# An attention and MLP kernel on one core: PV sums kept per pair of visits, their bank shared with QK, and a new order of maxima and exps

## The chip, the core and the metric

The kernel runs on one core of one Trainium2 chip. The metric is the device time of one launch in microseconds (us), as the median of several runs. The engines are called by the profile's names: PE is TensorE's matmul side and PEld its weight loads, DVE is VectorE, ACT is ScalarE, POOL is GpSimd, SP is SyncE, which issues nearly all DMAs.

## What is computed

The input is x of 2048 rows and 512 columns, in float32. It is normalised row by row, and two things are made of the result: attention with 32 heads of width 16, and a dense block of width 1792 with a squared ReLU. The second gates the first:

```python
xn = _layernorm(x, axis=-1)
s = _A_ref(xn, A_wqkv, A_wo)                # softmax(q k^T / 4) v, then wo
g = _silu(_B_ref(xn, B_w1, B_b1, B_w2, B_b2))   # relu(xn w1 + b1)^2 w2 + b2
return x + s * g
```

The attention is by far the larger part: 32 heads of 2048 by 2048 scores, which need a row maximum, an exp and a product with v. Most matmul operands are kept as a high and a low part, so that a product is three matmuls.

## The kernel before

**Units and steps.** The attention is cut into 32 units (`NU`): a unit is four heads (one "quad") by one chunk of 512 queries. A unit has 16 steps, one for each block of 128 keys. In a step, PE makes four score tiles of 128 keys by 512 queries (one for each head; `exp_mm`, matmul L1337), ACT turns each into exps (L1349, tile `pt`), and two steps later the PV matmuls (`pv_mm`, L453) multiply the exps by v. Since the exps need a row maximum that is known before, PE also makes every score tile a second time, transposed, 24 steps ahead (`LEAD`): `max_mm`, matmul L367, reduced by DVE (L374). These two kinds are called QK here, "s" for the exps' and "m" for the maxima's. So each step has four of each.

**Two lanes.** A QK matmul uses 64 of the array's 128 rows. Its partner on the other 64 rows ("lane" 0 or 1) is a matmul of the dense block (L268), made in the same way half by half, so that QK and dense matmuls run side by side. PV matmuls use all rows and 32 columns each, four side by side.

**Long slots.** `long_slots` writes out four steps by hand: 28 rounds, numbered r0 to r27, and three visits to PV. In 24 rounds a QK matmul on one lane stands beside a dense one on the other; first the 12 dense units of lane 0, then the 12 of lane 1. In the four rounds of `DOUBLE` both lanes hold QK. The string `ORDERS` tells which QK is "s" and which is "m". `VISITS` puts one step of PV after r11, one after r15 and two after r27. I call the rounds between the visits A (r0 to r11), B (r12 to r15) and C (r16 to r27). Between these blocks of four steps stand short slots, of one step, seven rounds and one step of PV, at the places where a dense sum does not divide by four.

**The fence.** Both lanes of a dense sum add into the same PSUM bank `pd_t`, and must not do so at once. So after the last dense unit of lane 0, in r12, `fence` (L1677) puts a wait into ACT's instructions: it waits for that matmul and sets a semaphore, on which lane 1's first dense matmul, in r15, waits. On ACT the fence stands behind whatever was issued before it, the exp of r12's own QK included, if that QK is an "s".

**Banks.** PSUM has eight banks of 128 by 512. Three (`se`) and three (`pm_t`) serve QK, one (`pd_t`) the dense sum, one (`po`) PV. The PV bank collects the 16 steps of a unit; then `evac` (L463) copies it on ACT into the SBUF tile `ot`, and a chain of DMAs and POOL operations (L502 to L504, `evac_norm`) divides by the sums over 14 steps. POOL waits there for the DMA `hl<-r_d`. Which QK gets which of the six banks is settled when the program is written: `flow` keeps a rough clock of PE, ACT and DVE (`ROUND`, `STEP`, `VISIT`, `READERS`), and each QK takes the bank that this clock says is free first, by preference one that the same reader had. On the chip a QK's weight load waits until the bank's last reader is through.

**Order.** In the loop all engines run in the order in which the code issues. POOL squares and splits the dense block's ReLU output (L618, L109, L110), splits the maxima and does `evac_norm`.

Of the kernel before, what the change touches and what calls it, by code (L numbers as in the profile page):

```python
# [9 lines left out]
F32 = mybir.dt.float32  # L10
F32R = mybir.dt.float32r
AF = mybir.ActivationFunctionType
# [50 lines left out]
READERS = {"s": (476, 675), "m": (600, 745), "d": (600, 755)}  # L63
EPS = 1e-5


# [1 line left out]
def kernel(  # L68
# [56 lines left out]
    with ExitStack() as ph:  # L125
# [136 lines left out]
        def block(mms, per, post, between={}):  # L262


            def emit(ms, lane, follow):
                r = slice(64 * lane, 64 * lane + 64)
                for out_, lh, rh, first_, last_ in ms:
                    mm = nc.tensor.matmul(  # L268
                        out_, lh(r), rh(r),
                        start=first_ and lane == 0, stop=last_ and lane == 1,  # L270
                        skip_group_check=True,
                    )
# [12 lines left out]
            assert len(units) == 12  # L285
            yield [
                [
                    lambda m=m, lane=lane, k=k: [
                        emit(m, lane, None if k else last_use[0]),
                        lane and k in between and between[k](),  # L290
                    ][0]
                    for k, m in enumerate(units)
                ]
                for lane in range(2)
            ], post, ORDERS[per == 1]

        def terms3(ps, terms):

# [37 lines left out]
        def flow_visit(n):  # L336
            flow["pe"] += VISIT + n * STEP
            flow["fresh"] = True

        def flow_take(kind):  # L340
            free = [i for i, spot in enumerate(spots) if spot[0] <= flow["pe"] and spot[2] == kind]
            at, t, _ = spots.pop(min(free or range(len(spots)), key=lambda i: spots[i][0]))
            flow["pe"] = max(flow["pe"], at)
            return t

        def flow_give(t, kind):
            every, held = READERS[kind]
            begin_ = max(flow[kind], flow["pe"] + READY)
            flow[kind] = begin_ + every
            spots.append([begin_ + held, t, kind])  # L350

        def flow_bank(kind):
            t = flow_take(kind)
# [94 lines left out]
                        ),  # L448
                    )

        def pv_mm(po, qd, kb, pts):
            for j in range(4):
                nc.tensor.matmul(  # L453
                    po[32 * j : 32 * j + 32, :],
                    vs[qd][:, (4 * kb + j) * VW : (4 * kb + j) * VW + 32], pts[j],
                    start=(kb == 0), stop=(kb == NT - 1), skip_group_check=True,
                )

        def evac(po, u):
            qd, qc = divmod(u, 4)  # L460
            cs = slice(qc * 512, (qc + 1) * 512)
            ot = sp.tile([P, 512], F32, name="ot", bufs=1)
            nc.scalar.activation(ot, po, AF.Copy)  # L463
            if u == NU - 3:
# [1073 lines left out]
        def pv_step(st, pts):  # L1538
            u, kb = divmod(st, 16)
            if kb == 0:  # L1540
                pos[0] = pv.tile([P, 512], F32, name="po")
            pv_mm(pos[0], u // 4, kb, pts)
            if kb == NT - 1:
                if u < NU - 2:
                    evac(pos[0], u)
                elif u == NU - 2:
                    unit_inner(pos[0])
                else:
                    unit_final(pos[0])

        def dense():
            mp = ExitStack()
# [111 lines left out]
                post()  # L1664
            max_end(g)

        def long_slots(st0, units, post, order):

            if not spots:
                flow_start((pe, "se", "s", 3), (pm, "pm_t", "m", 3))  # L1670
            todo = [[(st0 + k, j) for k in range(4) for j in (lane, lane + 2)] for lane in range(2)]
            for kb in range(st0, st0 + 4):
                pts.setdefault(kb, {})
            ops, st, pv_at = list(order), st0, st0 - 2

            def fence(mm):
                use = nc.scalar.nop()  # L1677
                tc.add_manual_dep(
                    use.ins, mm.ins.name,
                    mybir.DependencyInfo(  # L1680
                        mybir.DependencyClass.Sync, mybir.DependencyReason.DATA
                    ),
                    reason="the row tile is done with the bank",
                )
                last_use[0] = use

            def qk(lane):
                if ops.pop(0) == "m":
                    return max_mm(lane)
# [55 lines left out]
        for st_ in range(NU * 16):  # L1745
            if st_ < done:
                continue
            begin(st_)
            if st_ == FIRST:
                qs.close()  # L1750
            item = next(dn, None)
            if st_ == FIRST:

                for g in (LEAD, LEAD + 1):
                    max_end(g)
                for fn in last_store:
                    fn()
            if item is not None and len(item) > 2:
                assert st_ % 4 == 0
                long_slots(st_, *item)  # L1760
                done = st_ + 4
                to_visit[0] = st_ + 2
                continue
            wait = st_ >= LAST_MAX and item is not None and item[0] is not None and (st_ + flip[0]) % 2
            if item is not None and item[0] is not None:
                slot(st_, *item)
            else:

                plain_slot(st_)
                flip[0] += 1  # L1770
            shift_due(st_ + 1 + LEAD)
            if wait and (st_ - 2) % 16 != 15:
                continue
            for step in range(to_visit[0], st_ - 1):
                pv_step(step, pts.pop(step))
            flow_visit(st_ - 1 - to_visit[0])
            to_visit[0] = st_ - 1
        assert not [1 for it in stream for _ in it] and not left
        run_waiting(True)
        assert not waiting and next(dn, None) is None  # L1780
        flow["on"] = False
        for st_ in range(to_visit[0], NU * 16):
            pv_step(st_, pts.pop(st_))
        wstk.close()


# [24 lines left out]
```

## Time and profile before

| | us |
|---|---|
| median of 3 runs | 1616.87 |
| the runs | 1616.87, 1617.13, 1610.39 |
| profiled execution | 1610.35 |
| its span | 1608.6 |
| chain that ended last: matmul L453 (PV) | 30% of the span |
| the same, L268 (dense) | 13% |
| the same, L367 and L1337 on `pm_t` and `se` (QK) | 12%, 8%, 6% and 11% |

The granted clock of TensorE was full in all of the span. A row of the timeline gives the start and the length of an instruction or of several in a row (xN), both in us, the engine, the line, the operation, what it writes and reads, the shape, and in brackets how long the engine sat idle before and what ended that. A matmul on 64 rows is written 64\*128, one of PV 128\*32. The length of a matmul is modelled; the starts carry the argument. PV's matmuls are counted twice in the trace, 8 records for a step and 16 for two.

### The profile page before, as it was taken

The page shows a single profiled execution, that of the slowest core. Times are in us where ns is not written, and L with a number is a line of the kernel's source. Part 1 is how long each engine was busy: PE and PEld are TensorE (multiplying, and loading weights), DVE is VectorE, ACT ScalarE, POOL GpSimd, SP SyncE. Part 2 cuts the span into 40 slices and gives each one's busy share as a digit, 9 for nine tenths or more (in the row PEclk, how much of TensorE's full clock was granted, in tenths as well). Part 3 has the DMA queues.
Part 4 walks back from the last instruction along what each step waited for, and adds up shares of the span by engine and source line. Part 5 has one row for each costly group of instructions (what it writes and reads, how often), then busy time and mean ns, then how long its engine had stood idle before and what let it go on. Part 6 is the DMA issues. An engine that isn't in the chain of part 4 may idle for free.

```text
span 1608.6 us, 36225 instructions
## 1 busy us (share of the span) xinstructions
PE 1595.1 (99%) x13660; PEld 964.0 (60%) x13660; DVE 1345.8 (84%) x2307; ACT 1189.6 (74%) x2347; POOL 534.9 (33%) x610
## 2 busy tenths in 40 slices
PE   8999999999999999999999999999999999999998
PEld 7798665566546654665566456655665566545543
DVE  7486888888888888888888888888888888887764
ACT  7212777788778777887788778777877788778886
POOL 6436766233113311331133113311331134214621
PEclk9999999999999999999999999999999999999999
DMA  8977556435343433433434334433442253236755
GB/s 293 245 239 229 180 159 158 135 94 131 81 106 90 115 75 95 134 88 98 92 106 106 83 92 123 116 83 81 128 128 56 67 152 86 68 93 213 224 178 182
DMA packets 164174, 209.20 MB, mean 130 GB/s; under 512 B 59136, under 2 KB 79360, under 8 KB 162432
## 3 DMA queue, kind: packets, MB, share of 16 engines
q1 hardware_dynamic: 163856, 206.63, 46.4%
q8 instruction: 108, 1.77, 0.5%
q14 instruction: 66, 0.54, 0.1%
q10 hardware_dynamic: 144, 0.26, 0.0%
HBM read 148.90 MB, written 56.34 MB: 128 GB/s over the span
## 4 chain that ended last, share of the span: by engine, by line
PE 96%; DMA 1%; DVE 1%; issue 0%; SPq 0%; ACT 0%; POOL 0%; DVEq 0%
PE po L453 30%; PE pd_t L268 13%; PE pm_t L367 12%; PE se L1337 11%; PE se L367 8%; PE pm_t L1337 6%; PE pm_t L1206 4%; PE pd_t L236 4%; PE pm_t L236 2%; PE pd_t L1206 1%; PE se L1176 1%; PE se L1110 1%; PE pm_t L1297 0%; DVE mx L374 0%; PE se L236 0%
## 5 line engine op out<-in xcount | busy, mean ns | idle before, releaser
L374 DVE TENSOR_REDUCE mx<-pm_t 128x1 f32<-128x512 f32 x1236 | 799.2, 683 | 134.8 <-PE pd_t L268 82.4
L1349 ACT ACTIVATE pt<-se 128x512 f32<-128x512 f32 x1240 | 686.1, 606 | 182.8 <-PE pd_t L268 90.9
L374 DVE TENSOR_REDUCE mx<-se 128x1 f32<-128x512 f32 x795 | 528.5, 683 | 64.3 <-PE se L367 28.2
L1337 PE MATMUL se<-qe,ka 64*128 64x512 f32 x1346 | 530.4, 417 | 0.7 <-ACT pt L1349 0.7
L453 PE MATMUL po<-pt,v 128*32 128x512 f32 x3820 | 498.4, 602 | 0.2 <-DVE tsm L898 0.2
L367 PE MATMUL pm_t<-ka,qm 64*128 64x512 f32 x1236 | 480.4, 408 | 0.1
L1349 ACT ACTIVATE pt<-pm_t 128x512 f32<-128x512 f32 x666 | 388.9, 606 | 101.0 <-PE pd_t L268 58.5
L268 PE MATMUL pd_t<-xc,w1s 64*128 64x256 f32 x2352 | 328.8, 286 | 0.0
L1337 PEld LDWEIGHTS se<-qe,ka 64*128 64x128 f32 x1346 | 241.1, 184 | 137.1 <-ACT pt L1349 107.7
L367 PE MATMUL se<-ka,qm 64*128 64x512 f32 x795 | 310.6, 410 | 0.2
L268 PE MATMUL pd_t<-w2t,hT 64*128 64x512 f32 x1080 | 298.5, 408 | 0.0
L268 PEld LDWEIGHTS pd_t<-xc,w1s 64*128 64x128 f32 x2352 | 295.0, 186 | 0.0
L367 PEld LDWEIGHTS pm_t<-ka,qm 64*128 64x128 f32 x1236 | 222.9, 184 | 112.9 <-DVE mx L374 98.2
L1337 PE MATMUL pm_t<-qe,ka 64*128 64x512 f32 x695 | 283.6, 418 | 0.0
L453 PEld LDWEIGHTS po<-pt,v 128*32 128x32 f32 x3820 | 87.8, 108 | 158.7 <-issue 143.3
L268 PEld LDWEIGHTS pd_t<-w2t,hT 64*128 64x128 f32 x1080 | 180.9, 184 | 3.2
L367 PEld LDWEIGHTS se<-ka,qm 64*128 64x128 f32 x795 | 145.6, 184 | 51.5 <-DVE mx L374 36.0
L1337 PEld LDWEIGHTS pm_t<-qe,ka 64*128 64x128 f32 x695 | 126.3, 184 | 79.5 <-ACT pt L1349 64.4
L618 POOL TENSOR_TENSOR r<-r 128x512 f32<-128x512 f32 x56 | 58.2, 1039 | 321.1 <-ACT r L615 321.1
L502 POOL TENSOR_TENSOR ot<-ot,hl 128x512 f32<-128x512 f32 x27 | 34.7, 1286 | 154.5 <-DMA hl<-r_d 88.1
L637 POOL TENSOR_TENSOR u<-u,b_t 128x512 f32<-128x512 f32 x16 | 20.5, 1284 | 164.4 <-ACT u L636 164.4
L110 POOL TENSOR_TENSOR hT<-r,hT 128x512 fp32r<-128x512 f32 x56 | 72.5, 1295 | 4.7
(184 smaller groups left out, 1552.5 us busy)
## 6 DMA issues: line engine op xcount, KB each, us to landing
w1s<-w_d SPq DMA_DIRECT2D x196, 256.0 KB
qm<-q_d SPq DMA_DIRECT2D x384, 32.0 KB
ka<-k_d SPq DMA_DIRECT2D x96, 128.0 KB
qe<-q_d SPq DMA_DIRECT2D x384, 32.0 KB
q_d<-hl SPq DMA_DIRECT2D x16, 512.0 KB
g<-g_d SPq DMA_DIRECT2D x32, 256.0 KB
k_d<-hl SPq DMA_DIRECT2D x15, 512.0 KB
on_d<-hl SPq DMA_DIRECT2D x116, 64.0 KB
```

The lines of the kernel that those rows point to most:

```text
L110: (lo or nc.gpsimd).tensor_tensor(dst[1], raw, dst[0].bitcast(F32), op=ALU.subtract)
L236: mm = nc.tensor.matmul(out_, lh(r), rh(r), start=first_ and lane == 0, stop=last_ and lane == 1, skip_group_check=True,)
L268: mm = nc.tensor.matmul(out_, lh(r), rh(r), start=first_ and lane == 0, stop=last_ and lane == 1, skip_group_check=True,)
L367: nc.tensor.matmul(ps, qms[u][p][64 * j : 64 * j + 64, qb * P : (qb + 1) * P], kas[qd, p][64 * j : 64 * j + 64, kc * 512 : (kc + 1) * 512] ...
L374: return nc.vector.tensor_reduce(mxs[u][:, c, kc : kc + 1], ps, axis=AX.X, op=ALU.max)
L453: nc.tensor.matmul(po[32 * j : 32 * j + 32, :], vs[qd][:, (4 * kb + j) * VW : (4 * kb + j) * VW + 32], pts[j], start=(kb == 0), stop=(kb = ...
L502: nc.gpsimd.tensor_tensor(ot, ot, rb, op=ALU.mult)
L618: nc.gpsimd.tensor_tensor(r, r, r, op=ALU.mult)
L637: nc.gpsimd.tensor_tensor(u, u, b2_t, op=ALU.add)
L1206: mm = nc.tensor.matmul(out_, lh(r), rh(r), start=first_ and lane == first, stop=last_ and lane != first, skip_group_check=True,)
L1337: nc.tensor.matmul(se, kas[qd, j // 2][b : b + 64, kb * P : (kb + 1) * P], qes[u][j // 2][b : b + 64, :], start=True, stop=True,)
L1349: return nc.scalar.activation(pts[j], se, AF.Exp, scale=0.25)
```

## The change

In units 4 to 27 (`PARTS`) PV has no bank of its own. Its bank joins the six of QK, so that seven go round. A visit (`pv_visit`, new) takes a bank from the round, and its sum covers a pair of steps: the visit after r11 keeps its bank (`HELD`) and the one after r15 adds to it; the one after r27 is a pair by itself. Then ACT copies the bank into SBUF and gives it back. The first copy of a unit goes into the tile that holds the unit's sum (`ot` in odd units, one of three `ex` tiles in even ones), each other one into one of two more `ex` tiles by turns, and POOL adds it to the sum. In short slots each visit is of one step, and is copied and added by itself. The whole program then has 206 such copies and 182 additions, where it had 30 evacuations; 24 of these went. The rest of `evac` (now `evac_chain`) is as it was, and starts from the sum.

In long slots of these units the rounds with two QK are r0, r13, r14 and r16 instead of r11, r13, r14 and r27, and the order of "s" and "m" is another; there are 89 such slots. The clock of `flow` has new numbers. The other units keep their rounds and their PV bank.

```diff
-DOUBLE = (11, 13, 14, 27)
+DOUBLE = ((11, 13, 14, 27), (0, 13, 14, 16))
 VISITS = {12: 1, 16: 1, 28: 2}
+HELD = 12
-ORDERS = ("smsmsmsmsmssmmsmssmsmsmssmsmmmms", "smsmsmsmsmssmmsmssmsmsmssmsmmmms")
+ORDERS = ("smsmsmsmsmssmmsmssmsmsmssmsmmmms", "smsmsmsmmsssmsmssmmsmsmmsmssmmsm")
+PARTS = range(4, 28)
-STEP = 907
-VISIT = 185
+STEP = 858
+VISIT = 226
-READERS = {"s": (476, 675), "m": (600, 745), "d": (600, 755)}
+READERS = {"s": (476, 785), "m": (600, 855), "d": (600, 865)}
+VISIT_READY = 160
...
+        def flow_part(t):
+            begin_ = max(flow["s"], flow["pe"] + VISIT_READY)
+            flow["s"] = begin_ + READERS["s"][0]
+            spots.append([begin_ + READERS["s"][1], t, "s"])
...
+        def pv_visit(st, n, hold=False):
+
+            u, kb = divmod(st, 16)
+            if u not in PARTS:
+                for k in range(n):
+                    pv_step(st + k, pts.pop(st + k))
+                flow_visit(n)
+                return
+            if "shared" not in pos:
+                pos["shared"] = pv.tile([P, 512], F32, name="po")
+                spots.append([flow["pe"], pos["shared"], "s"])
+            first_ = "held" not in pos
+            po = flow_take("s") if first_ else pos.pop("held")
+            for k in range(n):
+                pv_mm(
+                    po, u // 4, kb + k, pts.pop(st + k),
+                    first_ and k == 0, not hold and k == n - 1,
+                )
+            flow_visit(n)
+            if hold:
+                pos["held"] = po
+                return
+            if kb == 0:
+                if u % 2:
+                    pos["sum"] = sp.tile([P, 512], F32, name="ot", bufs=1)
+                else:
+                    pos["sum"] = rot["ex"][0]
+                nc.scalar.activation(pos["sum"], po, AF.Copy)
+            else:
+                rot["ex"][1:] = rot["ex"][:0:-1]
+                part = rot["ex"][1]
+                nc.scalar.activation(part, po, AF.Copy)
+                nc.gpsimd.tensor_tensor(pos["sum"], pos["sum"], part, op=ALU.add)
+            flow_part(po)
+            if kb + n == NT:
+                evac_chain(pos["sum"], u)
...
-            ops, st, pv_at = list(order), st0, st0 - 2
+            parts = st0 // 16 in PARTS
+            double, order = DOUBLE[parts], ORDERS[parts]
+            ops, st, pv_at = list(order), st0, st0 - 2
...
-                if r in DOUBLE:
+                if r in double:
...
-                for _ in range(VISITS.get(r + 1, 0)):
-                    pv_step(pv_at, pts.pop(pv_at))
-                    pv_at += 1
                 if r + 1 in VISITS:
-                    flow_visit(VISITS[r + 1])
+                    pv_visit(pv_at, VISITS[r + 1], r + 1 == HELD)
+                    pv_at += VISITS[r + 1]
```

On PE, at the end of A in a long slot of units 4 to 27, before the change: L1337 is an "s", L367 an "m", L268 a dense matmul, L453 PV (`32x512` is one head's part).

```order
L1337 MATMUL se<-qe_739,ka_208 128x512
L268 MATMUL pd_t<-w2t,hT 128x512
L1337 MATMUL pm_t<-qe_738,ka_207 128x512
L367 MATMUL pm_t<-ka_208,qm_205 128x512
L453 MATMUL po<-pt_1493,v_1788 32x512
L453 MATMUL po<-pt_1485,v_1788 32x512
L453 MATMUL po<-pt_1492,v_1788 32x512
L453 MATMUL po<-pt_1490,v_1788 32x512
L367 MATMUL pm_t<-ka_208,qm_205 128x512
L268 MATMUL pd_t<-w2t,hT 128x512
L1337 MATMUL se<-qe_739,ka_208 128x512
L367 MATMUL se<-ka_208,qm_205 128x512
```

The same place of the changed program, where the lines are L1348 for an "s", L375 for an "m", L271 for dense and L461 for PV:

```order
L1348 MATMUL se<-qe_739,ka_208 128x512
L271 MATMUL pd_t<-w2t,hT 128x512
L375 MATMUL pm_t<-ka_208,qm_205 128x512
L271 MATMUL pd_t<-w2t,hT 128x512
L461 MATMUL pm_t<-pt_1491,v_1788 32x512
L461 MATMUL pm_t<-pt_1482,v_1788 32x512
L461 MATMUL pm_t<-pt_1478,v_1788 32x512
L461 MATMUL pm_t<-pt_1488,v_1788 32x512
L1348 MATMUL pm_t<-qe_738,ka_207 128x512
L271 MATMUL pd_t<-w2t,hT 128x512
L375 MATMUL se<-ka_208,qm_205 128x512
L1348 MATMUL se<-qe_739,ka_208 128x512 x2
```

The round before the visit held two QK and holds one and a dense matmul now; PV writes a bank that QK had a moment ago; and r12, the round with the last dense unit of lane 0, has become an "s" where it was an "m".

On ACT, before, around the ReLU of the dense block (L615) at the end of a long slot:

```order
L1349 ACTIVATE pt_1493<-se 128x512
L1349 ACTIVATE pt_1481<-se 128x512
L1349 ACTIVATE pt_1478<-pm_t 128x512
L615 ACTIVATE r_2403<-pd_t,b_t 128x256 x2
L1349 ACTIVATE pt_1494<-se 128x512
L1349 ACTIVATE pt_1482<-pm_t 128x512
```

The same in the changed program, where the ReLU is L626 and the copy of a pair of steps L1595:

```order
L1360 ACTIVATE pt_1479<-pm_t 128x512
L1360 ACTIVATE pt_1483<-po 128x512
L626 ACTIVATE r_2403<-pd_t,b_t 128x256 x2
L1595 ACTIVATE ex_1503<-se 128x512
L1360 ACTIVATE pt_1490<-pm_t 128x512
L1360 ACTIVATE pt_1484<-po 128x512
```

The copy stands behind the ReLU and ahead of all exps of the next slot, and exps now read the bank `po` too.

More of the change, by code (lines that the diff above doesn't have):

```diff
@@ L294, in block @@
                 for lane in range(2)
-            ], post, ORDERS[per == 1]
+            ], post, None
         def terms3(ps, terms):
@@ L347, in flow_give @@
             every, held = READERS[kind]
[L348 removed]
+            begin_ = max(flow[kind], flow["pe"] + READY + (FIRST_ROUND - ROUND if flow["fresh"] else 0))
             flow[kind] = begin_ + every
             spots.append([begin_ + held, t, kind])
+        def flow_part(t):
+            begin_ = max(flow["s"], flow["pe"] + VISIT_READY)
+            flow["s"] = begin_ + READERS["s"][0]
+            spots.append([begin_ + READERS["s"][1], t, "s"])
         def flow_bank(kind):
@@ L449, in shift_rows, with pv_mm @@
                     )
-        def pv_mm(po, qd, kb, pts):
+        def pv_mm(po, qd, kb, pts, first, last):
             for j in range(4):
@@ L455, in pv_mm @@
                     vs[qd][:, (4 * kb + j) * VW : (4 * kb + j) * VW + 32], pts[j],
-                    start=(kb == 0), stop=(kb == NT - 1), skip_group_check=True,
+                    start=first, stop=last, skip_group_check=True,
                 )
@@ L463, in evac, with evac_chain @@
             nc.scalar.activation(ot, po, AF.Copy)
+            evac_chain(ot, u)
+        def evac_chain(ot, u):
             if u == NU - 3:
@@ L1540, in pv_step @@
             if kb == 0:
+                if u - 1 in PARTS:
+                    spots[:] = [spot for spot in spots if spot[1] is not pos["shared"]]
                 pos[0] = pv.tile([P, 512], F32, name="po")
-            pv_mm(pos[0], u // 4, kb, pts)
+            pv_mm(pos[0], u // 4, kb, pts, kb == 0, kb == NT - 1)
             if kb == NT - 1:
@@ L1665, in slot, with long_slots @@
             max_end(g)
-        def long_slots(st0, units, post, order):
+        def long_slots(st0, units, post):
             if not spots:
@@ L1759 @@
                 assert st_ % 4 == 0
-                long_slots(st_, *item)
+                long_slots(st_, *item[:2])
                 done = st_ + 4
@@ L1773 @@
                 continue
-            for step in range(to_visit[0], st_ - 1):
-                pv_step(step, pts.pop(step))
-            flow_visit(st_ - 1 - to_visit[0])
+            pv_visit(to_visit[0], st_ - 1 - to_visit[0])
             to_visit[0] = st_ - 1
@@ L1782 @@
         for st_ in range(to_visit[0], NU * 16):
-            pv_step(st_, pts.pop(st_))
+            pv_visit(st_, 1)
         wstk.close()
```

## The prediction

> **What bounds the kernel now.** I read the page first: its busy times and the chain of work that ended last.
>
> ```profile
> span 1608.6 us, 36225 instructions
> PE 1595.1 (99%) x13660; PEld 964.0 (60%) x13660; DVE 1345.8 (84%) x2307; ACT 1189.6 (74%) x2347; POOL 534.9 (33%) x610
> PE 96%; DMA 1%; DVE 1%; issue 0%; SPq 0%; ACT 0%; POOL 0%; DVEq 0%
> ```
>
> PE sets the end nearly everywhere. But its matmuls' lengths are modelled, so time lost inside PE shows only in the distances between starts. So next I took the timeline of PE over one long slot, 784.19 to 795.42 (of each round one row is enough, of r11 and r27 both):
>
> ```profile
> 784.19 0.50 PE L1337 MATMUL se<-qe,ka 64*128 64x512 f32 x1
> 784.53 0.39 PE L367 MATMUL pm_t<-ka,qm 64*128 64x512 f32 x1
> 784.76 0.40 PE L1337 MATMUL pm_t<-qe,ka 64*128 64x512 f32 x1
> ...
> 786.64 0.39 PE L1337 MATMUL se<-qe,ka 64*128 64x512 f32 x1
> 786.88 0.47 PE L1337 MATMUL se<-qe,ka 64*128 64x512 f32 x1
> 786.90 0.49 PE L367 MATMUL se<-ka,qm 64*128 64x512 f32 x1
> 787.32 1.06 PE L453 MATMUL po<-pt,v 128*32 128x512 f32 x8
> 788.32 0.50 PE L367 MATMUL pm_t<-ka,qm 64*128 64x512 f32 x1
> ...
> 788.89 0.40 PE L1337 MATMUL se<-qe,ka 64*128 64x512 f32 x2
> 789.12 0.39 PE L268 MATMUL pd_t<-w2t,hT 64*128 64x512 f32 x1
> 789.44 1.06 PE L453 MATMUL po<-pt,v 128*32 128x512 f32 x8
> 790.44 0.49 PE L1337 MATMUL pm_t<-qe,ka 64*128 64x512 f32 x1
> 790.77 0.39 PE L367 MATMUL pm_t<-ka,qm 64*128 64x512 f32 x1
> ...
> 793.14 0.49 PE L1337 MATMUL se<-qe,ka 64*128 64x512 f32 x1
> 793.15 0.43 PE L367 MATMUL pm_t<-ka,qm 64*128 64x512 f32 x1
> 793.56 0.64 PE L453 MATMUL po<-pt,v 128*32 128x512 f32 x4
> ```
>
> A round takes 0.23 (784.53 to 784.76), the first after a visit 0.33 or 0.34. The last before a visit takes 0.32 in B (789.12 to 789.44), where it holds a QK and a dense matmul, but 0.44 in A (786.88 to 787.32) and 0.42 in C, where it holds two QK. Why, the weight loads tell:
>
> ```profile
> 786.41 0.19 PEld L1337 LDWEIGHTS se<-qe,ka 64*128 64x128 f32 x1
> 786.86 0.18 PEld L1337 LDWEIGHTS se<-qe,ka 64*128 64x128 f32 x1 [0.26 <-ACT pt L1349]
> 786.90 0.18 PEld L367 LDWEIGHTS se<-ka,qm 64*128 64x128 f32 x1
> 788.89 0.18 PEld L367 LDWEIGHTS se<-ka,qm 64*128 64x128 f32 x1
> 788.95 0.18 PEld L268 LDWEIGHTS pd_t<-w2t,hT 64*128 64x128 f32 x1
> ```
>
> The load for r10 ran 0.23 ahead of its matmul (786.41, 786.64), those for r15 0.17 and more. The loads for r11 came with their matmuls, since the bank was still being read by an exp. About 0.1 of a load then shows. So what PE loses is waiting for QK banks, at the ends of A and C, and 0.02 to 0.05 inside them.
>
> **The change part by part.** The 28 rounds and three visits of a long slot stay; the sum is made for one such slot, times 89.
>
> *Two QK no longer end A and C.* B shows a segment without such a wait: first round 0.33, last 0.32. With ten rounds of 0.233 between them, A and C would take 2.98. A takes 3.13 (784.19 to 787.32), C 3.12 (790.44 to 793.56): −0.15 and −0.14. Every fourth slot ends a unit, where ACT copies `po` after B today:
>
> ```profile
> 801.67 0.49 PE L1337 MATMUL se<-qe,ka 64*128 64x512 f32 x1
> 802.70 0.39 PE L1337 MATMUL se<-qe,ka 64*128 64x512 f32 x1
> 802.99 0.50 PE L1337 MATMUL se<-qe,ka 64*128 64x512 f32 x1
> 803.33 0.39 PE L367 MATMUL pm_t<-ka,qm 64*128 64x512 f32 x1
> 804.94 1.92 PE L453 MATMUL po<-pt,v 128*32 128x512 f32 x16
> 800.32 1.58 ACT L1349 ACTIVATE pt<-se 128x512 f32<-128x512 f32 x3 [0.82 <-PE se L1337]
> 801.85 0.60 ACT L463 ACTIVATE ot<-po 128x512 f32<-128x512 f32 x1
> 802.35 1.08 ACT L1349 ACTIVATE pt<-se 128x512 f32<-128x512 f32 x2
> ```
>
> There C takes 3.27, with rounds of 0.29 and 0.34 in the middle: the copy makes the first exp late and the six banks run out sooner. If the seventh bank covers that, another 0.15 in one slot of four: −0.04.
>
> *The seventh bank has to cover a copy after every pair.* So I counted A's 13 QK through by hand. Exps follow each other after 0.49 ((1.58 − 0.60) / 2 above) and last 0.60; maxima after 0.60 or 0.61 and last 0.68 (1.29 for two):
>
> ```profile
> 784.73 0.60 ACT L1349 ACTIVATE pt<-se 128x512 f32<-128x512 f32 x1 [1.62 <-PE pd_t L268]
> ...
> 807.55 1.29 DVE L374 TENSOR_REDUCE mx<-pm_t 128x1 f32<-128x512 f32 x2 [0.45 <-PE pd_t L268]
> ```
>
> A reader starts 0.54 after the first QK of a segment (784.19, 784.73), 0.45 after later ones. With the copy, ACT's first exp starts at 0.68 (801.67 to 802.35); I take 0.73, since the changed copy waits for PV in an instruction of its own. The QK of new A start at 0, 0, 0.33, 0.57, 0.80, 1.03, 1.27, 1.50, 1.73, 1.96, 2.20, 2.43, 2.66. Six banks are free at once, the seventh when the copy has read it (0.9, needed at 1.27). The 8th QK (1.50) then needs the first maximum's bank, back at 1.26; the 9th (1.73) the first exp's, 1.38; the 10th (1.96) the second exp's, 1.87; the 11th (2.20) the second maximum's, 1.86; the 12th (2.43) the third exp's, 2.36; the 13th (2.66) the third maximum's, 2.46. Each must be back 0.1 before its matmul. It falls short by at most 0.03, at the 10th and 12th. PV's own bank, the fourth exp's (2.85), is back at 2.98. The same count for today's A makes the two QK of r11 0.06 and 0.15 late, which is what the rows show, so I trust it to some 0.05. C comes out alike. I charge 0.03 for each of A and C: +0.06; the ends are 0 and 0.08 each.
>
> *New work.* 182 more copies of 0.60 on ACT, two for a slot: ACT then has 16 exps and the copies in a slot, 18 × 0.49 = 8.8 of 11.0, with the ReLU's 0.84 under 10. DVE has 16 × 0.60 = 9.6. Both stay under PE. POOL gets two additions for a slot, of the size of this one:
>
> ```profile
> 788.50 1.28 POOL L502 TENSOR_TENSOR ot<-ot,hl 128x512 f32<-128x512 f32 x1 [12.13 <-DMA hl<-r_d]
> ```
>
> 2 × 1.28 lies beside PE, as POOL is busy for a third. If that cover went, it would be rival 3. In the 28 short slots one copy each falls on ACT; nothing there says gain or loss, so 0, between −0.05 and +0.10 (−1.4 to +2.8 in all).
>
> *The fence.* In r12 an "s" stands now before the fence, so on ACT the fence comes behind that exp. Where the fence runs today, and whether a wait on ACT stands behind the exps ahead of it:
>
> ```profile
> L1677 ACTq EVENT_SEMAPHORE  x1: 17/17/17, 788.9 to 788.9; - x1
> L463 ACTq EVENT_SEMAPHORE  x1: 1217/1217/1217, 800.6 to 800.6; - x1
> L1349 ACT ACTIVATE pt<-se x3: 592/597/606, 800.3 to 801.3; 128x512 f32<-128x512 f32 x3
> ```
>
> The fence runs 0.6 after r12, and r15's dense load follows at 788.95. The copy's wait (L463) comes behind three exps in the program; it ran at 800.6, before the third had started (801.3). So ACT's waits run ahead of exps that are only queued, and the fence keeps its time: cost 0, at worst rival 2. The Trainium skill, Perfetto Trace Analysis, "DVE / Act Engine Instruction", says the same: once an instruction is pushed into the wait queue the sequencer takes the next. The Trainium skill's page TensorE: Matmul & The Clock Gate, "Architectural detail: the array is 16× 32×32, not 1× 128×128", calls ACT's queue "strict FIFO"; read so that the fence stands in it too, the sum would be rival 2's.
>
> *Sum.* −0.15 − 0.14 − 0.04 + 0.06 = −0.27 for a slot, times 89 is −24. Against the profiled execution, 1610.35 (1.75 outside its span), that is 1586. The median lies 6.5 above that execution, so I forecast 1616.87 − 24 = 1593. Without any bank wait it is −0.33, 1587.5; with 0.08 in each of A and C −0.17, 1602.
>
> **The rivals.**
>
> 1. *The wait only moves.* No slot today begins a segment with two QK, so what that costs isn't in the trace. If each such round shows 0.1 of load, as the late ones of A and C do, or the banks that the written clock picks are not the ones that come back first, 0.2 of the 0.27 goes: −6 us, 1611. For it: my count leaves no slack at two QK. Against it: r13, two QK in mid-segment, takes 0.24.
>
> 2. *The fence ends on ACT.* Place: r12 to r15. If the fence waits until ACT can start something behind r12's exp, it runs at 0.54 + 0.49 = 1.03; the load follows 0.05 later, and PV 0.42 after that load (786.90 to 787.32): B takes 1.50 instead of 1.12 (788.32 to 789.44). +0.38 against −0.27 is +0.11, +10 us, 1627. It decides once B grows by 0.27. Against it: 800.6.
>
> 3. *POOL holds ACT up.* POOL works in order and waits up to 12 for `hl<-r_d`. Additions behind that wait come late; a third copy waits for the tile of the first. If a unit loses 2.5 so, 24 units lose 60, 1653. Against it: two tiles are two pairs, about 11 us, and the wait ends at 788.50, between the visits of 787.32 and 789.44, ahead of that pair's copy.
>
> 4. *POOL slows DVE.* The Trainium skill, Perfetto Trace Analysis, "Optimizing Scalar/DVE Operations", says that both share an SBUF port and that moving work between them might not help. As a mechanism here: each addition holds the maxima for 1.28, DVE needs 9.6 + 2.6 = 12.2 a slot and becomes the bound, +1.0 for each, 1706. The rows say no:
>
> ```profile
> 811.45 1.29 DVE L374 TENSOR_REDUCE mx<-pm_t 128x1 f32<-128x512 f32 x2 [0.21 <-PE pd_t L268]
> 810.70 1.28 POOL L644 TENSOR_TENSOR u<-u,r 128x512 f32<-128x512 f32 x1
> ```
>
> Two maxima take 1.29 with POOL at work (811.45) as without it (807.55 above).
>
> **How the numbers follow.** The forecast has 0.71, rival 1 0.12 (half of it still faster by over 0.5%, half within), rival 2 0.10 (half within 0.5%, half slower), rival 3 0.05, rival 4 0.02. A difference of 0.5%, 8 us, is about what a measurement of this kernel can tell from none. Faster: 0.71 + 0.06 = 0.77; same: 0.06 + 0.05 = 0.11; slower: 0.05 + 0.07 = 0.12. The range starts at 1584, a little under the case without waits since the three runs lie 7 apart, and reaches to rival 1, 1611; rivals 2 to 4 and a tail of the forecast are left out.
>
> **What would show it.** In the changed profile A and C should take 2.98 to 3.06 with a last round of 0.33, B 1.13 with r15's load at 0.63 after r12, and the fence beside r12's running exp. Rival 1 shows as r0 to r1 over 0.4, or loads released by ACT or DVE; rival 2 as B of 1.5; rival 3 as copies (L1595) released by POOL; rival 4 as maxima longer than 0.68. B over 1.4 or a slot of 11.25 proves me wrong.

## The result and the profile after

| | before | changed |
|---|---|---|
| median of 4 runs, us | 1613.73 | 1595.56 |
| the runs | 1610.39 to 1617.13 | 1593.62 to 1597.82 |
| profiled execution | 1610.35 | 1595.43 |
| its span | 1608.6 | 1593.6 |

The ratio is 0.9888 (0.9857 to 0.9919): the change is faster by 18 us, 13 to 23. The forecast was 24 us less, 1593 (from the 1616.87 of the three runs known then). The profiled executions lie 14.9 apart, and what follows takes these 14.9 apart.

The page of the changed kernel, its span, busy times and the chain that ended last:

```profile
span 1593.6 us, 36834 instructions
PE 1577.9 (99%) x13660; PEld 971.4 (61%) x13660; DVE 1342.8 (84%) x2307; ACT 1272.5 (80%) x2529; POOL 766.8 (48%) x792
PE 94%; DMA 2%; DVE 1%; POOL 1%; SPq 1%; issue 1%; ACT 0%; DVEq 0%; POOLq 0%; ACTq 0%
```

ACT and POOL have more to do and PE still sets the end. Next, as before, the timeline of PE and its loads over a long slot, one whose dense matmuls are of the second layer (`w2t`), 788.96 to 799.89; r0 of A with its two QK, the last two rounds of A, the first and the last of C, PV, and the load of r11:

```profile
788.96 0.50 PE L1348 MATMUL se<-qe,ka 64*128 64x512 f32 x1
788.97 0.50 PE L375 MATMUL po<-ka,qm 64*128 64x512 f32 x1
...
791.39 0.39 PE L1348 MATMUL pm_t<-qe,ka 64*128 64x512 f32 x1
791.63 0.38 PE L375 MATMUL se<-ka,qm 64*128 64x512 f32 x1
791.94 1.06 PE L461 MATMUL pm_t<-pt,v 128*32 128x512 f32 x8
...
795.05 0.50 PE L1348 MATMUL pm_t<-qe,ka 64*128 64x512 f32 x1
...
797.71 0.39 PE L375 MATMUL se<-ka,qm 64*128 64x512 f32 x1
798.04 1.93 PE L461 MATMUL pm_t<-pt,v 128*32 128x512 f32 x16
...
791.47 0.18 PEld L375 LDWEIGHTS se<-ka,qm 64*128 64x128 f32 x1
```

A takes 2.98 (788.96 to 791.94) and C 2.99, where they took 3.13 and 3.12. The last round takes 0.31 and 0.33, and its load runs 0.16 ahead of its matmul (791.47, 791.63). Banks come back in time.

The same in a slot of the first layer (`w1s`), from r1 to PV after A. Such a round has two dense matmuls of 256 columns on one lane beside the QK on the other:

```profile
811.54 0.40 PE L1348 MATMUL se<-qe,ka 64*128 64x512 f32 x1
811.54 0.51 PE L271 MATMUL pd_t<-xc,w1s 64*128 64x256 f32 x3
...
813.89 0.39 PE L375 MATMUL se<-ka,qm 64*128 64x512 f32 x1
813.92 0.40 PE L271 MATMUL pd_t<-xc,w1s 64*128 64x256 f32 x2
814.25 0.64 PE L461 MATMUL pm_t<-pt,v 128*32 128x512 f32 x4
```

From r1 to r11 are ten rounds: the dense lane takes 2.38 for them (811.54 to 813.92), 0.238 each, in place of 0.233, and PV follows 0.33 after its last pair. A takes 3.06 (811.19 to 814.25).

From the starts of PV's and the rounds' first matmuls come these means of A, B and C, in us. Of the 89 slots 41 are of the second layer and 48 of the first:

| | A | B | C | whole slot |
|---|---|---|---|---|
| before, second layer | 3.133 | 1.126 | 3.173 | 11.279 |
| changed, second layer | 3.001 | 1.125 | 2.990 | 10.962 |
| before, first layer | 3.138 | 1.137 | 3.168 | 11.289 |
| changed, first layer | 3.063 | 1.158 | 3.067 | 11.133 |

That is 41 × −0.317 = −13.0 and 48 × −0.156 = −7.5, −20.5 together. The 28 short slots, each with its visit, took 81.9 and take 85.65: +3.7. Outside these slots 1.9 more is lost, nearly all of it after the last of them (179.8 before, 181.6 now). One wait there is new: DVE stands at the reciprocal of a unit's sums and waits for a DMA that SP issues late, and a load waits for the maximum behind it.

```profile
1479.29 3.66 SPq L751 DMA_DIRECT2D ts<-in_A_wo_dram  x8
1483.04 0.61 SPq L484 DMA_DIRECT2D sm<-ot  x1
...
1484.96 0.25 DVE L490 RECIPROCAL sm<-sm 128x16 f32<-128x16 f32 x1 [2.33 <-DMA sm<-ot]
1485.82 0.18 PEld L375 LDWEIGHTS pm_t<-ka,qm 64*128 64x128 f32 x1 [1.62 <-DVE mx L382]
```

−20.5 + 3.7 + 1.9 = −14.9.

### The profile page after: what moved, and what is told of

It reads as the page before. It is cut to its first block, busy times and chain, and to the rows that moved or that the text cites. A ratio compares the mean times of both kernels' runs of the same rounds, so it can differ in the third digit from the quotient of the medians.

```text
span 1593.6 us, 36834 instructions
## 1 busy us (share of the span) xinstructions
PE 1577.9 (99%) x13660; PEld 971.4 (61%) x13660; DVE 1342.8 (84%) x2307; ACT 1272.5 (80%) x2529; POOL 766.8 (48%) x792
## 4 chain that ended last, share of the span: by engine, by line
PE 94%; DMA 2%; DVE 1%; POOL 1%; SPq 1%; issue 1%; ACT 0%; DVEq 0%; POOLq 0%; ACTq 0%
PE pd_t L271 16%; PE po L461 11%; PE se L1348 9%; PE se L461 9%; PE pm_t L461 9%; PE pm_t L1348 8%; PE pm_t L375 7%; PE se L375 6%; PE pm_t L1217 4%; PE pd_t L239 3%; PE po L1348 2%; PE pm_t L239 1%; PE po L375 1%; PE pd_t L1217 1%; PE se L1187 1%; PE se L1121 1%
## 5 line engine op out<-in xcount | busy, mean ns | idle before, releaser
L382 DVE TENSOR_REDUCE mx<-pm_t 128x1 f32<-128x512 f32 x915 | 598.3, 682 | 80.4 <-PE pm_t L375 58.1
L1360 ACT ACTIVATE pt<-se 128x512 f32<-128x512 f32 x899 | 516.7, 616 | 42.8 <-PE pd_t L271 22.9
L1348 PE MATMUL se<-qe,ka 64*128 64x512 f32 x1005 | 393.5, 413 | 1.5 <-ACT pt L1360 1.5
L375 PE MATMUL pm_t<-ka,qm 64*128 64x512 f32 x915 | 356.6, 407 | 1.2 <-DVE mx L382 1.2
L375 PE MATMUL se<-ka,qm 64*128 64x512 f32 x896 | 339.9, 406 | 0.2
L1348 PE MATMUL pm_t<-qe,ka 64*128 64x512 f32 x820 | 320.9, 414 | 0.0
L271 PE MATMUL pd_t<-xc,w1s 64*128 64x256 f32 x2352 | 317.6, 282 | 0.0
L271 PEld LDWEIGHTS pd_t<-xc,w1s 64*128 64x128 f32 x2352 | 302.7, 187 | 2.4
L271 PE MATMUL pd_t<-w2t,hT 64*128 64x512 f32 x1080 | 285.5, 397 | 0.0
L1348 PEld LDWEIGHTS se<-qe,ka 64*128 64x128 f32 x1005 | 179.6, 184 | 127.4 <-ACT pt L1360 86.1
L1348 PEld LDWEIGHTS pm_t<-qe,ka 64*128 64x128 f32 x820 | 147.1, 184 | 118.2 <-ACT pt L1360 81.3
L1596 POOL TENSOR_TENSOR ot<-ot,ex 128x512 f32<-128x512 f32 x92 | 118.8, 1291 | 193.4 <-ACT ex L1595 193.2
L1596 POOL TENSOR_TENSOR ex<-ex,ex 128x512 f32<-128x512 f32 x90 | 116.2, 1292 | 185.2 <-ACT ex L1595 185.0
L271 PEld LDWEIGHTS pd_t<-w2t,hT 64*128 64x128 f32 x1080 | 193.2, 184 | 5.7
L375 PEld LDWEIGHTS pm_t<-ka,qm 64*128 64x128 f32 x915 | 166.0, 184 | 36.5 <-DVE mx L382 23.0
L375 PEld LDWEIGHTS se<-ka,qm 64*128 64x128 f32 x896 | 162.6, 184 | 40.4 <-DVE mx L382 28.1
L461 PE MATMUL pm_t<-pt,v 128*32 128x512 f32 x1328 | 168.8, 602 | 0.0
L461 PE MATMUL po<-pt,v 128*32 128x512 f32 x1212 | 166.9, 602 | 0.2 <-DVE tsm L909 0.2
L382 DVE TENSOR_REDUCE mx<-po 128x1 f32<-128x512 f32 x220 | 150.0, 682 | 17.2 <-PE po L375 13.9
L461 PE MATMUL se<-pt,v 128*32 128x512 f32 x1280 | 162.8, 602 | 0.0
```

The lines of the kernel that those rows point to most:

```text
L271: mm = nc.tensor.matmul(out_, lh(r), rh(r), start=first_ and lane == 0, stop=last_ and lane == 1, skip_group_check=True,)
L375: nc.tensor.matmul(ps, qms[u][p][64 * j : 64 * j + 64, qb * P : (qb + 1) * P], kas[qd, p][64 * j : 64 * j + 64, kc * 512 : (kc + 1) * 512] ...
L382: return nc.vector.tensor_reduce(mxs[u][:, c, kc : kc + 1], ps, axis=AX.X, op=ALU.max)
L461: nc.tensor.matmul(po[32 * j : 32 * j + 32, :], vs[qd][:, (4 * kb + j) * VW : (4 * kb + j) * VW + 32], pts[j], start=first, stop=last, ski ...
L1348: nc.tensor.matmul(se, kas[qd, j // 2][b : b + 64, kb * P : (kb + 1) * P], qes[u][j // 2][b : b + 64, :], start=True, stop=True,)
L1360: return nc.scalar.activation(pts[j], se, AF.Exp, scale=0.25)
```

## The experiments

Theory: PE loses only what it waits for banks. The seventh bank takes the waits out of the middle of A and C, and the new order those at their ends. Rivals: one of the two halves does it all; a pair of QK at the end costs by itself; POOL, not ACT, holds the short slots up. Means are over the slots named; "first" and "second" are the layers; the 28 short slots are summed, each with its visit. Each ratio goes by runs of the kernel before that were taken together with that run.

| | A, C second | A, C first | 28 short slots | median | ratio to before |
|---|---|---|---|---|---|
| changed | 3.00, 2.99 | 3.06, 3.07 | 85.65 | 1595.56 | 0.9888 (0.9857 to 0.9919) |
| order_only | 3.18, 3.18 | 3.18, 3.19 | 82.2 | 1616.68 | 1.0016 (1.0003 to 1.0028) |
| bank_only | 3.13, 3.13 | 3.13, 3.14 | 84.8 | 1615.17 | 1.0010 (0.9995 to 1.0025) |
| m_first | 3.00, 3.09 | 3.07, 3.10 | 85.2 | 1602.30 | 0.9932 (0.9912 to 0.9953) |
| half_first | 3.00, 2.99 | 3.00, 2.99 | 85.5 | 1583.97 | 0.9816 (0.9796 to 0.9835) |
| old_clock | 2.99, 3.04 | 3.06, 3.06 | 86.1 | 1598.65 | 0.9908 (0.9886 to 0.9930) |
| unheld | 2.99, 2.99 | 3.06, 3.07 | 85.1 | 1594.86 | 0.9883 (0.9864 to 0.9901) |
| no_adds | 3.00, 2.98 | 3.06, 3.07 | 85.9 | 1593.19 | 0.9870 (0.9844 to 0.9895) |
| hold_short | 3.00, 2.99 | 3.06, 3.07 | 82.5 | 1592.97 | 0.9870 (0.9844 to 0.9896) |
| hold_gate3 | 3.08, 2.99 | 3.06, 3.08 | 80.2 | 1591.85 | 0.9869 (0.9845 to 0.9893) |
| hold_gate4 | 2.99, 2.99 | 3.06, 3.10 | 80.2 | 1594.67 | 0.9883 (0.9862 to 0.9903) |
| gate_dve | 2.99, 2.99 | 3.06, 3.07 | 83.2 | 1592.03 | 0.9867 (0.9848 to 0.9886) |

### One half of the change at a time

order_only, on the kernel before:

```diff
-DOUBLE = (11, 13, 14, 27)
+DOUBLE = ((11, 13, 14, 27), (0, 13, 14, 16))
-ORDERS = ("smsmsmsmsmssmmsmssmsmsmssmsmmmms", "smsmsmsmsmssmmsmssmsmsmssmsmmmms")
+ORDERS = ("smsmsmsmsmssmmsmssmsmsmssmsmmmms", "smsmsmsmmsssmsmssmmsmsmmsmssmmsm")
+PARTS = range(4, 28)
...
+            parts = st0 // 16 in PARTS
+            double, order = DOUBLE[parts], ORDERS[parts]
...
-                if r in DOUBLE:
+                if r in double:
```

> The kernel before with only the new rounds and the new order of maxima and exps in units 4 to 27; PV keeps its own bank, six banks go round in QK. Theory (the seventh bank carries the gain): counted with six banks, the 7th QK of A comes 0.1 late and the 12th and 13th another 0.1 to 0.14, so A and C keep 3.08 to 3.15 and the time stays within 4 us of before. Rival (the order carries it, since a late load shows less when two QK start a segment): A and C fall to 3.06 or less in both kinds of slots and the time falls by 12 us or more.

Measured: A and C 3.18, and slower by 0.16% (0.03 to 0.28). The order alone brings nothing, as the theory has it, but 3.18 lies above the 3.08 to 3.15 that it gave. The count put the waits at the 7th, 12th and 13th QK of A (r5, r10 and r11); in the second layer r5, r7 and r9 take 0.26 (medians) and r10 0.34, and r11 waits for nothing. The timeline at the end of an A of the second layer (r10's load, then of r9, r10, r11 and PV the first matmul):

```profile
913.40 0.18 PEld L1338 LDWEIGHTS pm_t<-qe,ka 64*128 64x128 f32 x1 [0.16 <-DVE mx L375]
...
913.13 0.41 PE L1338 MATMUL se<-qe,ka 64*128 64x512 f32 x1
913.40 0.49 PE L1338 MATMUL pm_t<-qe,ka 64*128 64x512 f32 x1
913.73 0.39 PE L368 MATMUL se<-ka,qm 64*128 64x512 f32 x1
914.06 0.64 PE L454 MATMUL po<-pt,v 128*32 128x512 f32 x4
```

The last round is the 0.33 that a round without a wait takes there, but r9 takes 0.27 and r10 0.33, because r10's load starts with its matmul at 913.40, released by DVE.

bank_only, on the changed kernel:

```diff
-DOUBLE = ((11, 13, 14, 27), (0, 13, 14, 16))
+DOUBLE = ((11, 13, 14, 27), (11, 13, 14, 27))
-ORDERS = ("smsmsmsmsmssmmsmssmsmsmssmsmmmms", "smsmsmsmmsssmsmssmmsmsmmsmssmmsm")
+ORDERS = ("smsmsmsmsmssmmsmssmsmsmssmsmmmms", "smsmsmsmsmssmmsmssmsmsmssmsmmmms")
```

> The changed kernel with the old rounds (11, 13, 14, 27) and the old order in units 4 to 27; the bank is shared, pairs are copied and added as in the change. Theory (the bank carries the gain): the last two QK of A and C then find banks that are back in time, A and C stay within 0.03 of the changed kernel's 3.03, time 1592 to 1600. Rival (the order carries it): A and C go back to 3.13 and more, time 1610 or more.

My theory for this run failed: A and C are at 3.13 as before, and the time is not to be told from before's. But the middle changed. Before, rounds of 0.25 stood in A at r9 and in C at r21 and r23 (medians over the slots of the second layer); here all from r1 to r10 and from r17 to r26 take 0.22 to 0.24, and the last take 0.47 and 0.50. The timeline at the end of an A (896.35 to 899.47):

```profile
899.01 0.38 PE L1348 MATMUL pm_t<-qe,ka 64*128 64x512 f32 x1
899.04 0.49 PE L375 MATMUL pm_t<-ka,qm 64*128 64x512 f32 x1
899.47 0.64 PE L461 MATMUL po<-pt,v 128*32 128x512 f32 x4
...
899.04 0.18 PEld L375 LDWEIGHTS pm_t<-ka,qm 64*128 64x128 f32 x1
...
897.10 0.69 DVE L382 TENSOR_REDUCE mx<-se 128x1 f32<-128x512 f32 x1 [0.45 <-PE pd_t L271]
...
898.31 1.28 DVE L382 TENSOR_REDUCE mx<-pm_t 128x1 f32<-128x512 f32 x2
```

Only one of the last two QK is late. Its load starts at 899.04, 0.05 after the first of the two maxima of 898.31 ended (898.31 + 0.68 = 898.99). So all now hangs on a maximum's bank. In this order DVE's first maximum starts 0.75 after the start of A (897.10), in the changed kernel 0.57 (medians 0.77 and 0.57), because A begins with an exp's QK alone. If that is the cause, the place of the two QK doesn't matter. m_first tries this; it is bank_only with the first two letters of A (1 and 2) and of C (20 and 21) exchanged:

```diff
-ORDERS = ("smsmsmsmsmssmmsmssmsmsmssmsmmmms", "smsmsmsmsmssmmsmssmsmsmssmsmmmms")
+ORDERS = ("smsmsmsmsmssmmsmssmsmsmssmsmmmms", "mssmsmsmsmssmmsmssmmssmssmsmmmms")
```

> The changed kernel with the old rounds (11, 13, 14, 27), as in bank_only, and of the old order only the first two of A and of C exchanged: the first QK of each is for a maximum, the second for an exp. Theory (with seven banks the last QK of A and C waits for a maximum's bank, because DVE's first maximum starts at 0.78 after the start of A; with the maximum first it starts at 0.53, and three maxima later the bank is back 0.25 sooner): A and C of the slots of the second layer fall from bank_only's 3.13 to 3.05 or less, the time by 8 us or more. Rival (two QK at the end of a segment cost 0.13 whatever the banks do): A and C stay at 3.11 or more and the time within 3 us of bank_only.

Measured: A falls from 3.13 to 3.00, in the first layer to 3.07, just as in the changed kernel, with the two QK still in r11. C falls to 3.09, less than I expected. The whole is 13 us under bank_only. From its timeline the first and third maximum and the end of an A that starts at 891.92, then the end of a C:

```profile
892.46 0.69 DVE L382 TENSOR_REDUCE mx<-se 128x1 f32<-128x512 f32 x1 [0.22 <-PE pd_t L271]
893.76 1.28 DVE L382 TENSOR_REDUCE mx<-se 128x1 f32<-128x512 f32 x2
...
894.58 0.41 PE L375 MATMUL se<-ka,qm 64*128 64x512 f32 x1
894.91 0.64 PE L461 MATMUL pm_t<-pt,v 128*32 128x512 f32 x4
...
894.49 0.18 PEld L375 LDWEIGHTS se<-ka,qm 64*128 64x128 f32 x1
...
899.95 1.29 DVE L382 TENSOR_REDUCE mx<-se 128x1 f32<-128x512 f32 x2
900.70 0.18 PEld L1348 LDWEIGHTS se<-qe,ka 64*128 64x128 f32 x1
```

The first maximum starts at 0.54, the third ends at 894.44, and the load goes at 894.49, 0.09 ahead of its matmul: two QK at the end of A take 0.33. In C the last load still waits for a maximum (899.95 + 0.68 = 900.63; the load at 900.70). C's 13 QK are 7 for maxima, four of them in a row before the last; that these four are why C lags behind A I didn't try, so in C it is not shown that the two QK at the end cost nothing by themselves.

So neither half makes the kernel faster alone, and together they are worth 18 us. In the long slots the bank alone does save a little: C at the unit ends no longer stands out, and C in the second layer falls from 3.17 to 3.13; 3.1 go in the 89 slots, and the short slots take 2.9 of them back. With the early maximum but six banks A waits in r5 to r10; with seven banks but the late maximum it waits at the last QK. PV starts no earlier either way.

old_clock, on the changed kernel, asks what the bank that the written clock picks is worth:

```diff
-STEP = 858
-VISIT = 226
-READERS = {"s": (476, 785), "m": (600, 855), "d": (600, 865)}
+STEP = 907
+VISIT = 185
+READERS = {"s": (476, 675), "m": (600, 745), "d": (600, 755)}
```

> The changed kernel with the old numbers of the written clock (visit, step, readers), so that some QK take other banks. Theory (the banks are picked in nearly the same order, what counts is that there are seven): within 3 us of the changed kernel. Rival (the old numbers pick banks that are not back first): loads wait 0.1 or more in A and C, 9 us or more slower than the changed kernel.

Measured: 3 us more by the medians (the intervals overlap), 1.8 by the spans; C of the second layer is 3.04 instead of 2.99, 41 × 0.05 = 2. The numbers matter a little.

### The slots of the first layer

half_first, on the changed kernel, leaves out every second dense matmul there:

```diff
+            if per == 2:
+                units = [[u[k % 6 == 5]] for k, u in enumerate(units)]
```

> The changed kernel with one of the two dense matmuls left out in each round of the slots of the dense block's first layer (the slots with two 256-wide matmuls in a round; their result is then not the dense block's). Theory (in these slots the dense lane's own pace, 0.2385 for two matmuls against 0.2327 for a QK, sets A and C): A and C of these 48 slots fall from 3.06 to 2.99 or 3.00 as in the other 41, some 6 us less in all. Rival (banks come back late there, because ACT also runs the dense block's ReLU): A and C of these slots stay at 3.05 or more.

Measured: A and C of the 48 slots fall to 3.00 and 2.99. 48 × (0.067 + 0.081) is 7.1 of the 11.6 that go; 4.4 go in B (1.158 to 1.067, less than in the second layer), where after the lone matmul of 256 columns in r12 its lane goes on after 0.22, the other after 0.33. The timeline at the end of such an A (970.50 to 973.48):

```profile
973.02 0.38 PE L271 MATMUL pd_t<-xc,w1s 64*128 64x256 f32 x1
973.16 0.39 PE L377 MATMUL pm_t<-ka,qm 64*128 64x512 f32 x1
973.48 0.64 PE L463 MATMUL pm_t<-pt,v 128*32 128x512 f32 x4
```

Now PV follows the last QK by 0.32, as in the second layer. So in the changed kernel it was the pace of the dense lane, not a bank, that kept A and C at 3.06 there.

### Copies and additions

unheld copies each visit of a long slot by itself, three instead of two:

```diff
-HELD = 12
+HELD = 99
```

> The changed kernel with three copies in a long slot instead of two: the visit after r11 does not keep its bank, so each of the visits is copied, and POOL adds each up; 89 more copies and additions. ACT then has 16 exps and 3 copies, 20 operations with the ReLU, 20 x 0.49 = 9.8 of 11.1. Theory (copies lie beside PE, as ACT has room in the mean): B grows by at most 0.05, the time by 0 to 5 us. Rival (ACT has no room where the copy stands: its exps start 0.15 to 0.2 late after each visit and the banks with them): B grows by 0.1 to 0.2 and the time by 9 to 18 us.

Measured: nothing, 1594.86. 89 more copies on ACT and additions on POOL cost no time in long slots.

The short slots are another matter. no_adds:

```diff
-                nc.gpsimd.tensor_tensor(pos["sum"], pos["sum"], part, op=ALU.add)
```

> The changed kernel without the 182 additions on POOL (the later pairs are copied and then dropped). Theory (POOL holds ACT up in the short slots, and the later sum makes DVE wait for a DMA in the tail): the third and fourth short slot of a group fall from 2.05 and 2.28 to 3.56 to at most 1.95 and 2.0, the tail's wait of DVE goes, 4 to 5 us less than the changed kernel. Rival (ACT alone is too full there: 4 exps, a copy and the dense block's operation, 6 x 0.49 = 2.9 of 2.88): the short slots stay as they are and the time is within 1 us of the changed kernel, apart from the tail's 1.6.

The short slots stay at 85.9 in sum (the third of four groups fall to 2.0 or less, two of the fourth rise to 3.3 and 3.6), so the rival is right: POOL's additions are not what lengthens them. The tail's wait of DVE is gone in this run, and its time is 2.4 under the changed kernel's. But that wait is 1.8, 1.9 and 0.25 in hold_short, unheld and hold_gate3, which keep the additions, so they alone don't set it.

hold_short keeps the pairs in the short slots too:

```diff
-            pv_visit(to_visit[0], st_ - 1 - to_visit[0])
+            n = st_ - 1 - to_visit[0]
+            pv_visit(to_visit[0], n, n == 1 and to_visit[0] % 2 == 0)
```

> The changed kernel with the pairs kept in the short slots too: the first visit of two holds its bank, the second copies it, so 14 copies and 14 additions go. Theory (the copies and additions make the short slots longer): the 28 short slots without their visits take about 83 to 84 in place of 85.65, 2 to 3 us less than the changed kernel in all. Rival (with one bank held, six are left for QK, and the waits for banks take back what the copies gave): no less than the changed kernel.

Measured: 82.5 for the short slots, 3.1 less, and 3.0 less in the span. (The 85.65 of the expectation holds the visits too, though its words leave them out; 83 to 84 was meant in the same way.) The changed kernel's ACT in such a slot, the fourth of a group (PV of the one before at 1074.42, its own at 1077.70), with the load that waits:

```profile
1075.62 0.60 ACT L1595 ACTIVATE ex<-po 128x512 f32<-128x512 f32 x1 [0.39 <-PE po L461]
1076.11 0.62 ACT L653 ACTIVATE r<-u 128x512 f32<-128x512 f32 x1
1076.63 1.08 ACT L1360 ACTIVATE pt<-pm_t 128x512 f32<-128x512 f32 x2
...
1077.27 0.18 PEld L1348 LDWEIGHTS pm_t<-qe,ka 64*128 64x128 f32 x1 [0.41 <-ACT pt L1360]
```

Copy and tanh (L653) stand ahead of the first exp: it starts at 1076.63, 1.21 after the slot's first QK (1075.42) where 0.54 is usual, and the last QK waits for ACT. Without the copy these slots take 1.88 (2.28 with it). Against the changed kernel the intervals of the ratio overlap, so that hold_short is faster rests on the profile.

Two of the seven fourth slots still take 3.6 and 2.5 there. In them ACT waits 1.9 and 0.8 for POOL at the tanh. Three runs tried to move this, each on hold_short. hold_gate3:

```diff
-                    later(2, gate)
+                    later(3, gate)
```

> hold_short with the dense block's gate issued three steps after its sum instead of two. Theory (in the fourth short slot of some groups ACT stands at the gate's tanh, waiting for POOL's addition, and the exps behind it come late: 3.6 and 2.5 where the others take 1.88): those two slots lose their extra, and 1.5 to 2.5 us go. Rival (the tanh only takes its time and its wait elsewhere): within 1 us of hold_short.

hold_gate4:

```diff
-                    later(2, gate)
+                    later(4, gate)
```

> hold_short with the dense block's gate issued four steps after its sum instead of two. Theory: as with three steps, 1.5 to 2.5 us less than hold_short, and the waits in B of the first long slot after a group, 0.2 to 0.27 each, change with it. Rival: within 1 us of hold_short.

gate_dve:

```diff
-                    nc.gpsimd.tensor_tensor(u, u, b2_t, op=ALU.add)
+                    nc.vector.tensor_tensor(u, u, b2_t, op=ALU.add)
```

> hold_short with the 16 additions of the dense block's bias moved from POOL to DVE, so that ACT's tanh two steps later does not stand behind POOL's norm and additions. Theory (the two fourth short slots of 3.6 and 2.5 come from ACT waiting for that addition on POOL): they fall to 1.88 and some 2 us less than hold_short; the waits in B of the first long slot after a group, where ACT waits for no one, stay. Rival (16 more operations of 0.6 to 1.3 on DVE, which is busy 84% of the time, hold the maxima up): 0.2 or more for each of the 16, the time no less than hold_short's.

With three steps the short slots lose 2.3, as expected, but the tanh then stands behind the copy at the head of the next long slot, whose A takes 3.48 to 3.77, seven times. hold_gate3's ACT and loads there (A begins at 1076.14):

```profile
1076.34 0.60 ACT L1595 ACTIVATE ex<-se 128x512 f32<-128x512 f32 x1 [0.43 <-PE se L461]
1076.83 0.62 ACT L653 ACTIVATE r<-u 128x512 f32<-128x512 f32 x1
1077.35 0.59 ACT L1360 ACTIVATE pt<-se 128x512 f32<-128x512 f32 x1
...
1077.99 0.18 PEld L375 LDWEIGHTS se<-ka,qm 64*128 64x128 f32 x1 [0.35 <-ACT pt L1360]
1078.48 0.18 PEld L1348 LDWEIGHTS pm_t<-qe,ka 64*128 64x128 f32 x1 [0.30 <-ACT pt L1360]
```

With four steps other segments pay: B 1.184 in the second layer, C 3.10 in the first. In gate_dve the two slots come down to 1.98 and 1.95, and the third ones go up, to between 2.05 and 3.03. By the medians the three lie 1.1 below, 1.7 above and 0.9 below hold_short, not quite within the 1 us that the rivals of the first two gave, nor is gate_dve's time "no less". The rivals held in kind: the waits moved.

## Why the prediction was nearly right

- **What bounds the kernel: right.** PE waits for QK banks at the ends of A and C.
- **"Two QK no longer end A and C", −0.15 and −0.14: right in size for the second layer, wrong as a cause in A.** A and C fell by 0.13 and 0.18 (with the unit ends in it), but m_first gets A's share with the two QK still at its end. In C m_first gets from bank_only's 3.13 to 3.09 only; which part of the order brings it to 2.99 isn't shown. What the new order brings is a maximum in the first round. The prediction's hand count had that (the first maximum's bank "back at 1.26"), its words did not.
- **"Ten rounds of 0.233": wrong for 48 of the 89 slots.** The slot I read was of the second layer. Those of the first have a dense pair of 0.240 in each round (means; 0.233 in the second); that is 0.07 or 0.08 for each of A and C, 7 us. This is the step that failed. It stood in the trace of before, had I counted one slot of each layer: there, in a slot that starts at 818.07, the dense matmuls of r1 and r10 lie nine rounds and 2.16 apart, 0.240 each.

```profile
818.41 0.40 PE L268 MATMUL pd_t<-xc,w1s 64*128 64x256 f32 x2
820.57 0.40 PE L268 MATMUL pd_t<-xc,w1s 64*128 64x256 f32 x2
```

- **Unit ends, −0.04: right.** C no longer stands out there, in bank_only neither, so this is the seventh bank's part.
- **Waits in the new A and C, +0.06: too high** in the second layer, where A and C are at 2.99 to 3.00.
- **The fence, 0: right.** In the changed kernel's timeline r12 starts at 792.94, its exp at 793.47, the fence runs at 793.5 while that exp lasts, and r15's load goes at 793.57. B is 1.125 in the second layer.

```profile
793.47 0.60 ACT L1360 ACTIVATE pt<-pm_t 128x512 f32<-128x512 f32 x1 [0.29 <-PE pd_t L271]
L1729 ACTq EVENT_SEMAPHORE  x1: 17/17/17, 793.5 to 793.5; - x1
793.57 0.18 PEld L271 LDWEIGHTS pd_t<-w2t,hT 64*128 64x128 f32 x1
```

- **Copies beside PE in long slots: right**, and there was room for 89 more (unheld).
- **Short slots, 0, between −1.4 and +2.8: wrong, +3.7.** I put each copy beside PE by ACT's mean load. But a short slot of 2.88 with its visit has four exps and a copy, some with a tanh or the dense block's copy: 6 × 0.49 = 2.9. ACT has no room there, and there the copy shows.
- **The tail, not foreseen, +1.9.** ACT copies into `ot` at 1466.28, but SP issues `sm<-ot` only 16.8 later, behind eight DMAs that it issues one after another; it lands 1.9 after that. Before, it was issued 14.0 after the copy and DVE didn't wait. Why SP is so far behind stays open, and it isn't all: the stretch after the last of these slots takes 179.4 to 183.8 in the kernels here, DVE's wait lies between 0 and 3.4, and the two don't go together (m_first has 181.9 with a wait of 0.5). So differences of 2 us between runs may lie there.
- **Rivals.** None took over. Part of 3 shows: four copies wait 0.2 each for POOL, and three fourth short slots (3.56, 2.55 and 2.51, the others 2.28) have a tanh that waits for POOL; before had one of 2.82. In B of six slots, each the first of the first layer, the fourth after a group of short slots, 0.2 to 0.27 is lost, 1.4 us, and goes elsewhere when the tanh is moved. Rival 4: the maxima take 0.68 as before.

With 41 slots at −0.32 and 48 at −0.16 the sum for the long slots is −20.5 in place of −24: the second layer gave 2 us more than forecast, the first 5.5 less. The copies and the tail took 5.6 of it. That 1595.56 lies only 2.6 above the 1593 is partly luck: with the fourth run the kernel before has a median 3.1 lower than the one I started from, and the fall is 18 by the medians and 15 by the profiled executions, not 24.

## What to carry to other kernels

A wait that shows at the end of a stage may have two causes in a row, and taking away one only uncovers the other: try the halves of a change alone before saying which one works. Count one stage of each kind, not one stage times all. An engine's room is to be read in the shortest stage in which it gets the new work, not in its mean.

## What the runs showed of the hardware

gate_dve showed a contention that I had not met in the maxima. From its timeline, DVE's addition of two SBUF tiles (0.69 in the median of 16) beside POOL's work:

```profile
915.39 1.66 DVE L648 TENSOR_TENSOR u<-u,b_t 128x512 f32<-128x512 f32 x1
...
915.21 1.29 POOL L513 TENSOR_TENSOR ot<-ot,hl 128x512 f32<-128x512 f32 x1 [3.56 <-DMA hl<-r_d]
916.58 0.94 POOL L514 TENSOR_SCALAR hl<-ot 128x512 fp32r<-128x512 f32 x1
```

POOL's addition had begun first and kept its 1.29; DVE's took 1.66 instead of 0.69, and ended 0.55 after POOL's. Then POOL's next operation took 0.94 instead of the usual 0.62. Another, at 604.46, 0.83 after the start of a POOL operation, took 1.00 and also ended 0.55 after it. Both lie in the third short slot of a group, the ones that take 3.03 and 2.37. The Trainium skill, Perfetto Trace Analysis, "Optimizing Scalar/DVE Operations", says that the two share an SBUF read port; these rows agree. The maxima, which read PSUM, don't feel it: in the changed kernel the 174 that run wholly beside one of the 182 additions take 0.68, like the others.

And in the changed kernel two matmuls of 256 columns on one lane take 0.240 where one of 512 takes 0.233 (means over A and C): 0.007 for a matmul more, enough to make A and C 0.07 longer over ten rounds.
